# Pooled attention and a top-1 mixture of experts: the routing scratch in another PSUM bank, wider row spacing in the routing table, four buffers of x and two of the exponentials

## The chip, the core and the metric

The kernel runs on one core of a Trainium2 chip. The metric is device time in microseconds (us) of a whole execution.

## What is computed

The reference, cut to what matters:

```
# attention: 8 batches, 8 heads, 576 tokens, 64 per head
k_p = k.reshape(B, H, 72, 8, D).mean(axis=3)      # keys and values are
v_p = v.reshape(B, H, 72, 8, D).mean(axis=3)      # averaged by eights
attn = softmax(q @ k_p.T / 8);  o = attn @ v_p
x = o, as 4608 tokens of 512 numbers
# mixture of experts
out = x.copy()
xc = x[x @ w_skip > 0]                            # about half of the tokens
e_idx, gate_w = top 1 of softmax(xc @ w_gate)     # one of 8 experts
h = relu(xc @ w1[e]);  y = gate_w * (h @ w2[e])   # 512 -> 1024 -> 512
out[computed tokens] = xc + y
```

## The kernel before

**Two stages.** `attention` works through 36 tiles of 128 tokens (the loop at L633), writes each tile's x to `out` in DRAM (L367), and routes the tokens meanwhile. `experts` then takes, for each expert, its tokens out of `out` again, runs the two layers in products of a high and a low half of each number (L1075 to L1093), and scatters the sums back. Between the two, `slots` (L791) works out which tokens each expert gets, in units of 128 slots.

**A tile's way.** The attention is pipelined over the tiles: in the turn of tile t, TensorE does the scores of t (L299), the transposes of the exponentials of t-2 (L324 into the PSUM tile `pt`, L328 into `pr`), and the value products of t-4 (L342, L344) into `o`. VectorE takes the minimum of t's negated scores (L306); ScalarE does eight exponentials of t-1, one for each head (L313), and copies `pt` and `pr` to SBUF (L325, L329); VectorE normalises tile t-5 out of `o` (`rs` L359, `rc` L361, the routing logits L365, x L366), and SyncE issues the transfer of that x to `out` (L367). `x` has three buffers, so the write of a tile's x needs the transfer of the x three tiles before to have landed; `e` (the exponentials) has three as well. `o` is one buffer of two PSUM banks, so the value products of the next tile (L342) wait for L366.

**PSUM.** Eight banks: three for scores, one for `pr`, one (`mps`) that the small jobs share, one for `pt`, two for `o`. The bank of `pr` is cut in two: columns 0 to 255 hold the transposes of L328, columns 256 to 511 are the scratch of the routing. The scheduler orders accesses bank by bank: who writes into `pr` waits for a VectorE access to the scratch, though the columns differ.

**Routing.** `route` (L373) works in six groups of 9, 9, 7, 6, 3 and 2 tiles. VectorE sums the logits of the heads and finds each token's expert, in some ten small operations on the scratch, up to the one-hot `r_oh` (L401). In the next turn ScalarE takes the exponentials of the logits (`r_ex`, L403) and TensorE counts, by products with a triangle and with ones (L407, L409) into an `mps` tile, each token's rank among those of its expert. VectorE adds the running counts (L410, L411) and, one turn on, forms the token's row of the table (`r_di`, L421): expert x 4608 + rank. GpSimd then writes for each tile of the group the pair of token number and gate to these rows, by an indirect DMA of 128 times 8 bytes (L426). Tokens that skip have a row out of bounds and are not written. The table lies in DRAM. After the last group, L842 gathers 128 rows each of it, transposes turn them into the slot numbers (L873, L874), and the first tokens are gathered by these (L876).

**Values of a batch.** `pool_v` (L226) sums values by eights on GpSimd (L234 to L236), transposes the sums (L259, L260) and multiplies them by the gate's weights (L268, L269), both into `mps` tiles, and spreads them into `vbd` and `vl` (L276, L279), which the value products read.

**Order.** On TensorE, ScalarE and VectorE the instructions run in the order in which the program writes them; on GpSimd and on SyncE's queue the scheduler sets the order. `weights` loads expert 0's weights between the tiles and splits them into halves (L550 on ScalarE, the rest L552 on VectorE or L554 on GpSimd). In the last two turns (t = 34 and 35) `tx` (L482) transposes two early tiles of tokens for expert 0, so that its work can begin while the tail of the attention and the routing run out.

The lines in question:

```
side_ps = ps_p.tile([128, 4, 128], F32, name="pr")                      # L186
pr, scratch = side_ps[:, 0:2], flat(side_ps)[:, 256:512]                # L187
rk = flat(ps_m.tile([128, 4, 128], F32, name="mps"))[:, 0:(n + 1) * NE] # L405
m = nc.gpsimd.indirect_dma_start(table, bass.IndirectOffsetOnAxis(ap=di[:, j:j + 1], axis=0),
                                 pay[:, t0 + j, :], None, ...)          # L425
```

Of the kernel before, what the change touches and what calls it, by code (L numbers as in the profile page):

```python
# [26 lines left out]
F32 = mybir.dt.float32  # L27
F32R = mybir.dt.float32r
BF16 = mybir.dt.bfloat16
I32 = mybir.dt.int32  # L30
AF = mybir.ActivationFunctionType
ALU = mybir.AluOpType
# [4 lines left out]
B, H, S, HD, POOL = 8, 8, 576, 64, 8  # L37
SP = S // POOL
D = H * HD
NTOK = B * S  # L40
NT = NTOK // 128
NE, F = 8, 1024
JT = NTOK // 128
MAXU = NT // 2 + NE - 1
UNITS = MAXU + 2
# [57 lines left out]
def flat(ap):  # L103
    return ap.rearrange("p k n -> p (k n)")
# [56 lines left out]
def attention(tc, nc, q, k, vm, vr, cf, w1, w2, whi, wlo, out, c, pay, offs, table, load_constants, near, bufs, late, early, fin):  # L161
    with ExitStack() as ctx:
# [20 lines left out]
        nc.gpsimd.memset(init[:, 512:], 0.0)  # L183
        l8s = {}

        side_ps = ps_p.tile([128, 4, 128], F32, name="pr")  # L186
        pr, scratch = side_ps[:, 0:2], flat(side_ps)[:, 256:512]  # L187

# [37 lines left out]
        def pool_v(b, vt, vl):  # L226
# [28 lines left out]
            for _ in range(SUMS[min(b, 2)]):  # L255
                yield
            tp = ps_m.tile([128, 4, 128], F32, name="mps")
            for j in range(2):
# [5 lines left out]
            if b:  # L264
                yield
            gp = ps_m.tile([128, 512], F32, name="mps")
            for j in range(2):
# [42 lines left out]
        def exped(sc, nm):  # L310
            e = ap.tile([128, H, SP], F32, name="e", bufs=3)
            for h in range(H):
                nc.scalar.activation(e[:, h, :], sc[h // 4][:, h % 4 * SP:(h % 4 + 1) * SP], AF.Exp,  # L313
                                     bias=nm[:, h:h + 1], scale=-1.0)
            return e
# [31 lines left out]
        def normalised(t, os):  # L347
            x = ap.tile([128, H, HD], F32, name="x", bufs=3)
            t0 = max(a for a in starts if a <= t)
# [23 lines left out]
        def route(t0, n):  # L373
# [11 lines left out]
            mx = new("r_mx"); no = new("r_no"); cn = new("r_cn"); oh = new("r_oh", NE, dt=BF16)  # L385
            ex = new("r_ex", NE); sn = new("r_sn"); di = new("r_di", dt=I32)
            nc.vector.tensor_reduce(lp, l8s.pop(t0)[:, :n].rearrange("p j h c -> p j c h"), axis=AX.X, op=ALU.add)
# [16 lines left out]

            rk = flat(ps_m.tile([128, 4, 128], F32, name="mps"))[:, 0:(n + 1) * NE].rearrange("p (j e) -> p j e", e=NE)  # L405
            for j in range(n):
# [13 lines left out]
            yield  # L420
            nc.vector.tensor_tensor(di, ds, no, ALU.add)  # L421
            yield
            nc.vector.reciprocal(pay[:, t0:t0 + n, 1], sn)
# [43 lines left out]
        def tile_steps():  # L467
# [13 lines left out]

            def tx(land, i):  # L482
                ps = flat(ps_t.tile([128, 4, 128], F32, name="pt") if i % 2 else ps_m.tile([128, 4, 128], F32, name="mps"))
                sl = slice(i * 128, i * 128 + 128)
                for k in range(4):
                    nc.tensor.transpose(ps[:, k * 128:k * 128 + 128], land[:, k * 128:k * 128 + 128], ident)
                pv = ps.rearrange("p (k n) -> p k n", k=4)
                nc.scalar.activation(xhi[:, :, sl], pv, AF.Copy)
                return lambda: nc.vector.tensor_tensor(xlo[:, :, sl], pv, xhi[:, :, sl].bitcast(F32), ALU.subtract)
# [143 lines left out]
        for t in range(NT):  # L633
# [35 lines left out]
            if t >= NT - 2:  # L669
                assert not later  # L670
                if t == NT - 2:
                    tx, steps = tile_steps()
                low = tx(bufs["ring"][:, t - NT + 5], t - NT + 2)
            nm = ap.tile([128, H], F32, name="nm")
# [116 lines left out]
def slots(tc, nc, c, offs, table, near, bufs, out, fin, p, psum):  # L791
# [6 lines left out]
    none = new("none"); kind = new("kind"); slim = new("slim")  # L798
    ends = p.tile([128, H, SP], F32, name="e", bufs=3).rearrange("p h k -> p (h k)")[:, 0:UNITS * NE].rearrange("p (u e) -> p u e", e=NE)
    row = p.tile([128, UNITS], F32, name="s_row", bufs=1)  # L800
# [477 lines left out]
```

## Time and profile before

| what | us |
|---|---|
| three runs | 553.86, 556.23, 557.14 |
| median | 556.23 |
| profiled execution | 556.37 |
| its span, first to last instruction | 554.6 |

A profile is of one execution. Its span is 1.8 us shorter than that execution's own time; the rest is start and end around the instructions. PE is TensorE, DVE VectorE, ACT ScalarE, POOL GpSimd, and SP SyncE. A name with a q (SPq, POOLq) is the same engine where it issues transfers. The windows view gives for a stretch of the span its length, the busy time of PE, PE's weight loads, DVE, ACT and POOL with the count of instructions, then the clock that the throttle granted TensorE (1.00 is full speed), the mean busy share of the sixteen DMA engines, and GB/s. A row of the timeline gives start, duration, engine, line, operation, output and inputs; in brackets stands how long the engine had sat idle and who ended that. A row of the waits view says who waited for whose result, and in how many us in all, how many times, and the longest. The view of DMA issues gives count, size and the median time from issue to landing.

### The profile page before, as it was taken

Reading aid. Unit: us, or ns where it says so; the run is one execution under the profiler, and the core shown is the slowest. Engines: PE = TensorE matmul, PEld = TensorE weight load, DVE = VectorE, ACT = ScalarE, POOL = GpSimd, SP = SyncE. Lnnn points to the kernel's source line nnn. Section 1 sums busy time; section 2 is a strip of 40 time slices with the busy share of each in tenths; the row PEclk is TensorE's granted clock in tenths of the full one; section 3 lists DMA queues with packets and bytes.
Section 4 is the critical chain, followed back from the end, with each engine's and each line's share of the span. In section 5 each row is a group of like instructions: output and inputs, shape, how many; then the busy total and the mean of one; then the engine's idle time right before and its main releaser. Section 6 shows DMA issues by size and latency. Waiting matters only on the chain. (4 is left out here: it accounts for less than half of the span.)

```text
span 554.6 us, 11051 instructions
## 1 busy us (share of the span) xinstructions
PE 513.1 (93%) x3346; PEld 460.4 (83%) x3347; DVE 298.7 (54%) x696; ACT 244.7 (44%) x671; POOL 215.7 (39%) x293
## 2 busy tenths in 40 slices
PE   6799997898899969999999999999999999999994
PEld 3699796797788758798989898998989898989893
DVE  4577776876777622235632653233254657565563
ACT  5588796799661112123412341122244445443441
POOL 5764547669836423121422132323232043314042
PEclk8799999999899978999999999999999999999997
DMA  8989899788952011015421442102144637462200
GB/s 292 389 293 338 278 289 262 275 304 167 306 121 76 12 33 48 23 58 173 146 95 57 170 155 78 57 38 68 61 170 144 223 125 272 153 226 100 97 27 7
DMA packets 33591, 86.03 MB, mean 155 GB/s; under 512 B 7501, under 2 KB 7762, under 8 KB 31760
## 3 DMA queue, kind: packets, MB, share of 16 engines
q1 hardware_dynamic: 25456, 71.62, 39.3%
q0 software_dynamic: 8096, 13.95, 7.8%
q8 instruction: 18, 0.29, 0.2%
q14 instruction: 21, 0.17, 0.1%
HBM read 73.79 MB, written 20.52 MB: 170 GB/s over the span
## 5 line engine op out<-in xcount | busy, mean ns | idle before, releaser
L1075 PE MATMUL psl<-xhi,w1hi 128*128 128x256 f32 (+3 forms) x416 | 123.4, 297 | 5.1 <-PEq L905 3.8
L1076 PE MATMUL psl<-xlo,w1hi 128*128 128x256 f32 (+3 forms) x416 | 122.6, 295 | 0.0
L1077 PE MATMUL psl<-xhi,w1lo 128*128 128x256 f32 (+3 forms) x416 | 122.5, 294 | 0.0
L1131 ACT ACTIVATE hhi<-psl 128x256 fp32r<-128x256 f32 (+4 forms) x104 | 42.0, 404 | 159.6 <-ACTq L905 158.5
L994 POOL DMA_INDIRECT out<-ring,slot x39 | 39.7, 1019 | 184.5 <-POOLq L905 173.8
L1090 PE MATMUL psf<-w2hi,hhi 128*128 128x512 f32 x240 | 96.1, 400 | 2.5 <-issue 1.3
L1091 PE MATMUL psf<-w2lo,hhi 128*128 128x512 f32 x240 | 94.9, 395 | 0.0
L1188 DVE SCALAR_TENSOR_TENSOR hlo<-psl,hhi 128x256 fp32r<-128x256 f32 (+2 forms) x104 | 43.8, 423 | 82.0 <-DVEq L905 81.5
L1075 PEld LDWEIGHTS psl<-xhi,w1hi 128*128 128x128 f32 x416 | 79.5, 191 | 7.1 <-issue 6.5
L1076 PEld LDWEIGHTS psl<-xlo,w1hi 128*128 128x128 f32 x416 | 79.6, 191 | 0.5
L1077 PEld LDWEIGHTS psl<-xhi,w1lo 128*128 128x128 f32 x416 | 79.4, 191 | 0.0
L1093 PE MATMUL psf<-w2hi,hlo 128*128 128x512 f32 x200 | 79.1, 395 | 0.0
L313 ACT ACTIVATE e<-sc,nm 128x72 f32<-128x72 f32 x288 | 65.3, 353 | 1.0 <-DVE nm L306 0.8
L1177 DVE SCALAR_TENSOR_TENSOR ring<-psf,ring 128x512 f32 x25 | 18.7, 749 | 78.7 <-DVEq L905 78.7
L342 PE MATMUL o<-vbd,pT 128*128 128x148 f32 (+1 forms) x304 | 49.6, 300 | 6.8 <-DVE x L366 4.2
L1090 PEld LDWEIGHTS psf<-w2hi,hhi 128*128 128x128 f32 x240 | 45.1, 188 | 12.7 <-issue 2.9
L1091 PEld LDWEIGHTS psf<-w2lo,hhi 128*128 128x128 f32 x240 | 45.1, 188 | 9.7
L989 POOL DMA_INDIRECT ring<-out,slot x39 | 45.0, 1154 | 15.6 <-issue 13.4
L1140 ACT ACTIVATE xhi<-psd 128x512 fp32r<-128x512 f32 x36 | 18.9, 598 | 70.5 <-ACTq L905 70.5
L342 PEld LDWEIGHTS o<-vbd,pT 128*128 128x128 f32 (+1 forms) x304 | 41.3, 184 | 8.4 <-issue 4.5
L1093 PEld LDWEIGHTS psf<-w2hi,hlo 128*128 128x128 f32 x200 | 37.6, 188 | 9.1
L426 POOL DMA_INDIRECT table<-pay,r_di x36 | 35.7, 990 | 22.3 <-DVE rc L361 9.9
(218 smaller groups left out, 863.6 us busy)
## 6 DMA issues: line engine op xcount, KB each, us to landing
stage<-in_w SPq DMA_DIRECT2D x64, 512.0 KB, 4.3
out<-x SPq DMA_DIRECT2D x36, 256.0 KB, 5.9
stage<-in_k SPq DMA_DIRECT2D x6, 1152.0 KB, 10.3
hlo<-in_vm SPq DMA_DIRECT2D x4, 1024.0 KB, 7.9
hhi<-in_vm SPq DMA_DIRECT2D x4, 1024.0 KB, 8.4
xlo<-in_q SPq DMA_DIRECT2D x6, 512.0 KB, 8.1
qt<-in_q SPq DMA_DIRECT2D x6, 512.0 KB, 8.1
xhi<-in_q SPq DMA_DIRECT2D x5, 512.0 KB, 12.0
```

What stands on the lines that cost most here:

```text
L313: nc.scalar.activation(e[:, h, :], sc[h // 4][:, h % 4 * SP:(h % 4 + 1) * SP], AF.Exp, bias=nm[:, h:h + 1], scale=-1.0)
L342: nc.tensor.matmul(o_[sl, g * 2 * VA:(g + 1) * 2 * VA], pT[:, 2 * a + g, sl], vbd[b % 3][:, 2 * a + g, :], start=(g == 0), stop=False)
L989: g.indirect_dma_start(ring[:, s % 6, 0:D], None, out, bass.IndirectOffsetOnAxis(ap=slot[:, s:s + 1], axis=0), bounds_check=NTOK - 1, oob_ ...
L994: g.indirect_dma_start(out, bass.IndirectOffsetOnAxis(ap=offsets, axis=0), ring[:, s % 6, 0:D], None, bounds_check=NTOK - 1, oob_is_err=Fa ...
L1075: t.matmul(ps, whi[0][:, k, w], xhi[:, k, xs], start=(k == 0), stop=False)
L1076: t.matmul(ps, whi[0][:, k, w], xlo[:, k, xs], start=False, stop=False)
L1077: last = t.matmul(ps, wlo[0][:, k, w], xhi[:, k, xs], start=False, stop=(k == 3))
L1090: t.matmul(ps, hhi[:, k, sl], whi[1][:, k, :], start=(k == 0), stop=False)
L1091: last = t.matmul(ps, hhi[:, k, sl], wlo[1][:, k, :], start=False, stop=(short and k == 7))
L1093: last = t.matmul(ps, hlo[:, k, sl], whi[1][:, k, :], start=False, stop=(k == 7))
L1131: a.activation(hhi[:, f, xs], psL[f % 3][:, xs], AF.Relu).then_inc(sem["act"], 1)
L1188: m = v.scalar_tensor_tensor(to[:, f], psL[f % 3][:, cs], 0.0, hhi[:, f, cs].bitcast(F32), ALU.max, ALU.subtract)
```

## The change

Four edits:

1. **Banks.** The bank of `pr` now holds the transposes of L328 alone. The routing scratch moves to the bank of `mps`, which becomes one tile, `side_ps`, that lives through the attention: the value batches' transposes lie in its columns 0 to 383, their gate products and the rank products at its start, the routing scratch in the last 180 columns. The early `tx` of the last two turns takes the `pt` bank both times.
2. **Rows of the table.** Each row number is changed by two more VectorE operations for each group: row r becomes r xor ((r mod 4) x 8). A row of 8 bytes moves by 0, 8, 16 or 24 rows, that is by multiples of 64 bytes, so rows that follow each other in rank no longer share 64 bytes; every aligned stretch of 32 rows stays a stretch of the same 32.
3. **Buffers of x:** four instead of three.
4. **Buffers of the exponentials `e`:** two instead of three.

```
-        side_ps = ps_p.tile([128, 4, 128], F32, name="pr")
-        pr, scratch = side_ps[:, 0:2], flat(side_ps)[:, 256:512]
+        pr = ps_p.tile([128, 4, 128], F32, name="pr")[:, 0:2]
+        side_ps = ps_m.tile([128, 512], F32, name="mps")
+        scratch = side_ps[:, 512 - GMAX * 20:]
...
-            tp = ps_m.tile([128, 4, 128], F32, name="mps")
+            tp = side_ps[:, 0:384].rearrange("p (j n) -> p j n", j=3)
...
-            gp = ps_m.tile([128, 512], F32, name="mps")
+            gp = side_ps
...
-            e = ap.tile([128, H, SP], F32, name="e", bufs=3)
+            e = ap.tile([128, H, SP], F32, name="e")
...
-            x = ap.tile([128, H, HD], F32, name="x", bufs=3)
+            x = ap.tile([128, H, HD], F32, name="x", bufs=4)
...
-            rk = flat(ps_m.tile([128, 4, 128], F32, name="mps"))[:, 0:(n + 1) * NE].rearrange(...)
+            rk = side_ps[:, 0:(n + 1) * NE].rearrange(...)
...
             nc.vector.tensor_tensor(di, ds, no, ALU.add)
+            nc.vector.tensor_scalar(dx, di, 3, 3, ALU.bitwise_and, ALU.logical_shift_left)
+            nc.vector.tensor_tensor(di, di, dx, ALU.bitwise_xor)
...
-            def tx(land, i):
-                ps = flat(ps_t.tile(..., name="pt") if i % 2 else ps_m.tile(..., name="mps"))
+            def tx(land, i, early=False):
+                ps = flat(ps_t.tile(..., name="pt") if early or i % 2 else ps_m.tile(..., name="mps"))
```

The order on TensorE, ScalarE and VectorE stays, apart from the new operations on VectorE; the semaphores that instructions wait on change with the banks, and GpSimd's order moves in places. TensorE in the turn in which the first routing group does its first steps on VectorE, before (names: `pt` and `pr` take the transposes of the exponentials, `cfs` holds the identity, `kbd` the keys, `vbd` and `vl` the values):

```order
L324 MATMUL pt<-cfs,e 128x128 [waits Activation_49]
L324 MATMUL pt<-cfs,e 128x128 x3
L328 MATMUL pr<-cfs,e 128x128 [waits DVE_49,Activation_49]
L328 MATMUL pr<-cfs,e 128x128
L299 MATMUL sc<-kbd_115,xlo 128x144 [waits Activation_49]
L299 MATMUL sc<-kbd_115,xlo 128x144
L342 MATMUL o<-vbd_123,pT 128x148 [waits DVE_49,PE_49]
```

The same place with the change, where every line number from here on is one higher or more:

```order
L325 MATMUL pt<-cfs,e 128x128 [waits Activation_49]
L325 MATMUL pt<-cfs,e 128x128 x3
L329 MATMUL pr<-cfs,e 128x128 [waits Activation_49]
L329 MATMUL pr<-cfs,e 128x128
L300 MATMUL sc<-kbd_115,xlo 128x144 [waits DVE_49,Activation_49]
L300 MATMUL sc<-kbd_115,xlo 128x144
L343 MATMUL o<-vbd_123,pT 128x148 [waits DVE_49,PE_49]
```

The transposes into `pr` have lost their wait on VectorE; the second half of the scores, which follows them, now names VectorE itself. Later in the same turn and into the next come the rank products on TensorE, before:

```order
L344 MATMUL o<-vl_126,p_791 128x148
L299 MATMUL sc<-kbd_115,xlo 128x144 [waits Activation_49]
L299 MATMUL sc<-kbd_115,xlo 128x144
L407 LDWEIGHTS ones
L407 MATMUL mps<-r_oh,ones 128x80 [waits DVE_49]
```

And with the change:

```order
L345 MATMUL o<-vl_126,p_787 128x148
L300 MATMUL sc<-kbd_115,xlo 128x144 [waits Activation_49]
L300 MATMUL sc<-kbd_115,xlo 128x144
L408 LDWEIGHTS ones
L408 MATMUL mps<-r_oh,ones 128x80 [waits Activation_49]
```

The first rank product waited on VectorE, which writes the one-hot `r_oh`; it now waits on ScalarE, whose `r_ex` (L403) reads the scratch in the bank into which the product writes. The third place is GpSimd at the sums of value batch 6 (`hlo` and `vl` hold the loaded values, `w1lo` the low half of a weight chunk), before:

```order
L279 TENSOR_TENSOR vl_125<-gs,cfs 64x4x9 [waits Activation_49]
L234 TENSOR_TENSOR hlo<-hlo 128x256 [waits DMAHW4_49]
L234 TENSOR_TENSOR hlo<-hlo 128x256 x3
L234 TENSOR_TENSOR vl<-vl 64x256 [waits DMAHW5_49]
L235 TENSOR_TENSOR hlo<-hlo 128x512 [waits Pool_49]
L235 TENSOR_TENSOR vl<-vl 64x128 [waits Pool_49]
L554 TENSOR_TENSOR w1lo<-stage,w1hi 128x512 [waits DMAHW1_49,Activation_49]
L236 TENSOR_TENSOR vs<-hlo 128x256 [waits PE_49,Pool_49]
```

And with the change:

```order
L280 TENSOR_TENSOR vl_125<-gs,cfs 64x4x9 [waits Activation_49]
L558 TENSOR_TENSOR w1lo<-stage,w1hi 128x512 [waits DMAHW1_49,Activation_49]
L235 TENSOR_TENSOR hlo<-hlo 128x256 [waits DMAHW4_49]
L235 TENSOR_TENSOR hlo<-hlo 128x256 x3
L235 TENSOR_TENSOR vl<-vl 64x256 [waits DMAHW5_49]
L236 TENSOR_TENSOR hlo<-hlo 128x512 [waits Pool_49]
L236 TENSOR_TENSOR vl<-vl 64x128 [waits Pool_49]
L237 TENSOR_TENSOR vs<-hlo 128x256 [waits PE_49,Pool_49]
```

The split of a weight chunk into halves (L554, L558 with the change) now stands ahead of the batch's sums instead of among them. The other moves are of the same kind: a low half of w2 between the sums of batch 7, one scatter of the first group ahead of a low half of w2.

More of the change, by code (lines that the diff above doesn't have):

```diff
@@ L385, in route @@
             mx = new("r_mx"); no = new("r_no"); cn = new("r_cn"); oh = new("r_oh", NE, dt=BF16)
-            ex = new("r_ex", NE); sn = new("r_sn"); di = new("r_di", dt=I32)
+            ex = new("r_ex", NE); sn = new("r_sn"); di = new("r_di", dt=I32); dx = new("r_dx", dt=I32)
             nc.vector.tensor_reduce(lp, l8s.pop(t0)[:, :n].rearrange("p j h c -> p j c h"), axis=AX.X, op=ALU.add)
@@ L403, in route @@
             nc.scalar.activation(ex, l, AF.Exp)
-            rk = flat(ps_m.tile([128, 4, 128], F32, name="mps"))[:, 0:(n + 1) * NE].rearrange("p (j e) -> p j e", e=NE)
+            rk = side_ps[:, 0:(n + 1) * NE].rearrange("p (j e) -> p j e", e=NE)
             for j in range(n):
@@ L480, in bank @@
                 return hold["ps"]
-            def tx(land, i):
-                ps = flat(ps_t.tile([128, 4, 128], F32, name="pt") if i % 2 else ps_m.tile([128, 4, 128], F32, name="mps"))
+            def tx(land, i, early=False):
+                ps = flat(ps_t.tile([128, 4, 128], F32, name="pt") if early or i % 2 else ps_m.tile([128, 4, 128], F32, name="mps"))
                 sl = slice(i * 128, i * 128 + 128)
@@ L672, in attention @@
                     tx, steps = tile_steps()
-                low = tx(bufs["ring"][:, t - NT + 5], t - NT + 2)
+                low = tx(bufs["ring"][:, t - NT + 5], t - NT + 2, True)
             nm = ap.tile([128, H], F32, name="nm")
@@ L798, in slots @@
     none = new("none"); kind = new("kind"); slim = new("slim")
-    ends = p.tile([128, H, SP], F32, name="e", bufs=3).rearrange("p h k -> p (h k)")[:, 0:UNITS * NE].rearrange("p (u e) -> p u e", e=NE)
+    ends = p.tile([128, H, SP], F32, name="e").rearrange("p h k -> p (h k)")[:, 0:UNITS * NE].rearrange("p (u e) -> p u e", e=NE)
     row = p.tile([128, UNITS], F32, name="s_row", bufs=1)
```

## Prediction

> **What bounds the kernel now.** I read the page first, for the shares of the engines.
>
> ```profile
> span 554.6 us, 11051 instructions
> PE 513.1 (93%) x3346; PEld 460.4 (83%) x3347; DVE 298.7 (54%) x696; ACT 244.7 (44%) x671; POOL 215.7 (39%) x293
> ```
>
> TensorE is the engine that sets the time: busy for 513.1 of 554.6 us, the next one for 298.7. So an edit is worth what it takes from TensorE's idle time or slow time. The windows tell the two stages apart.
>
> ```profile
> 0.00:204.70 204.70, 175.61 (x1302) 155.99 (x1303) 138.51 (x425) 130.06 (x475) 121.04 (x175) 0.95 0.73 233
> 204.70:554.60 349.90, 337.49 (x2044) 304.38 (x2044) 160.20 (x271) 114.68 (x196) 94.66 (x118) 0.98 0.32 110
> ```
>
> The change touches the first stage alone. There TensorE is idle for 204.7 - 175.6 = 29.1 us, and its clock is 0.95 instead of the 0.98 of the second stage. Next, the waits, of which these are TensorE's in the middle of the stage.
>
> ```profile
> PE o L342 <- DVE x L366: 4.2, 1, 4.2
> ...
> PE pr L328 <- DVE l L365: 2.7, 3, 1.0
> PE pr L328 <- DVE rs L359: 2.7, 2, 1.4
> PE o L342 <- POOL vbd L276: 2.6, 1, 2.6
> PE pr L328 <- DVE pr L410: 2.3, 2, 1.6
> ```
>
> One wait of 4.2 us on the normalised x, one of 2.6 us on GpSimd's values, and seven waits of the transposes into `pr` on VectorE, 2.7 + 2.7 + 2.3 = 7.7 us in all. The change is aimed at the first and the third.
>
> **Four buffers of x.** The timeline shows what stood behind the 4.2 us, and the line of the transfers says how old it was.
>
> ```profile
> 94.36 0.69 DVE L366 TENSOR_TENSOR x<-o,rc 128x512 f32<-128x512 f32 x1 [4.57 <-DMA out<-x]
> ...
> 95.20 0.83 PE L342 MATMUL o<-vbd,pT 128*128 128x148 f32 x2 [4.16 <-DVE x L366]
> ```
>
> ```profile
> L367 SPq DMA_DIRECT2D out<-x x1: 344/344/344, 79.5 to 79.5; - x1
> ...
> DMA to landing us min/median/max: 14.8/14.8/14.8
> ```
>
> VectorE wanted to write x at 94.36 - 4.57 = 89.8 and had to wait for the transfer issued at 79.5, which landed at 79.5 + 14.8 = 94.3. With four buffers this write needs an older transfer, and the wait is gone. Late next is the write one tile on, which now needs the transfer that lands at 94.3. How long a tile takes is in the row of all x writes of this stretch.
>
> ```profile
> L366 DVE TENSOR_TENSOR x<-o,rc x16: 680/681/692, 63.8 to 127.3; 128x512 f32<-128x512 f32 x16
> ```
>
> Fifteen turns in 63.5 us, less the stall of 4.2 and some 1.5 of slow clock (below), are 3.85 us each. The next write comes at 89.8 + 3.85 = 93.65 and waits 0.65. VectorE had 0.4 us to spare ahead of TensorE (4.57 against 4.16), so 0.25 of that reaches TensorE. The stall gives 4.16 - 0.25 = 3.9 us. It also drags the clock:
>
> ```profile
> 91.40:94.80 3.40, 0.00 (x0) 0.00 (x0) 0.44 (x1) 1.04 (x3) 2.76 (x7) 1.00 0.93 217
> 94.80:98.20 3.40, 3.00 (x12) 2.97 (x12) 2.24 (x5) 1.69 (x6) 0.00 (x0) 0.50 1.01 400
> 139.20:142.60 3.40, 0.80 (x7) 0.68 (x6) 3.15 (x4) 2.23 (x9) 3.40 (x6) 1.00 0.77 220
> 142.60:146.00 3.40, 3.40 (x16) 3.39 (x15) 3.30 (x8) 0.00 (x0) 3.02 (x3) 0.50 0.99 337
> ```
>
> After 3.4 us without a matmul the clock is 0.50 for the next 3.4 us, in which 3.00 us of busy time are worth 1.5. With the stall gone that is 1.5 us more: the edit gives 5.4. Its bounds: 2.5, if another transfer is late by 2 us or more in place of this one and the slow clock stays, and 5.7, if nothing waits.
>
> The last two rows show the same after the stall on `vbd`, with 0.80 us of work in the window before. The Trainium skill (TensorE: Matmul & The Clock Gate, Part 1, What's actually happening) says that the slow clock follows on one whole idle window of about 3.4 us, of a grid that runs free. By that rule the rows at 139.2 would have brought no slow clock; the trace shows 0.50 after 2.6 idle us, so the measurement decides.
>
> For the sum it matters that such windows start every 3.4 us while everything after 95 us now comes some 5 us earlier. The stall on `vbd` can fall otherwise into them, and its slow clock (1.7) go; or another pause can catch one. I take no change, and 1.7 either way as a bound.
>
> **The bank of `pr` alone.** It removes VectorE's waits ahead of L328, 7.7 us. But see what TensorE does after such a wait.
>
> ```profile
> 104.02 0.68 DVE L366 TENSOR_TENSOR x<-o,rc 128x512 f32<-128x512 f32 x1
> 104.11 0.41 PE L328 MATMUL pr<-cfs,e 128*128 128x128 f32 x2 [0.96 <-DVE l L365]
> ...
> 104.85 0.35 PE L342 MATMUL o<-vbd,pT 128*128 128x148 f32 x1
> ```
>
> The transposes had waited 0.96. Then follow the scores, and L342 at 104.85, which cannot start before L366 has ended, at 104.02 + 0.68 = 104.70. Had L328 started 0.96 earlier, L342 would still have waited for 104.70: gain 0.15. The longest wait, 1.62, ends so:
>
> ```profile
> 109.43 0.16 DVE L411 TENSOR_TENSOR offs<-offs,mps 128x8 f32<-128x8 f32 x1
> 109.45 0.44 PE L328 MATMUL pr<-cfs,e 128*128 128x128 f32 x2 [1.62 <-DVE pr L410]
> 109.74 0.41 PE L259 MATMUL mps<-cfs,vs 128*128 128x128 f32 x2
> ```
>
> L259, right behind, writes `mps`, which L411 reads until 109.59: it would stop there, 0.15 earlier than now. The other five are of the same kind: they stand in turns in which VectorE is late with its routing steps, and the next value products wait for VectorE's x in any case. I count 0.3 for all seven; the bounds are 0 and 7.7, and the two that can be followed, with 0.3 of 2.58, are near the lower.
>
> **The new wait.** The rank products write into the bank that ScalarE reads for `r_ex`, so they now come behind it, as the order shows. Before, of the first three groups:
>
> ```profile
> 66.56 0.28 ACT L403 ACTIVATE r_ex<-pr 128x72 f32<-128x72 f32 x1
> 66.68 0.37 PE L407 MATMUL mps<-r_oh,ones 128*128 128x80 bf16 x8
> ```
>
> ```profile
> 106.92 0.40 PE L407 MATMUL mps<-r_oh,ones 128*128 128x80 bf16 x9
> 107.04 0.29 ACT L403 ACTIVATE r_ex<-pr 128x72 f32<-128x72 f32 x1
> ```
>
> ```profile
> 136.68 0.34 PE L407 MATMUL mps<-r_oh,ones 128*128 128x64 bf16 x7
> 137.66 0.27 ACT L403 ACTIVATE r_ex<-pr 128x56 f32<-128x56 f32 x1
> ...
> 141.92 0.64 PE L342 MATMUL o<-vbd,pT 128*128 128x148 f32 x3 [2.60 <-POOL vbd L276]
> ```
>
> `r_ex` ended 0.16 after the start of the products in the first group (66.84 against 66.68), 0.41 in the second and 1.25 in the third. TensorE's queue stands behind the rank products: the transposes of the exponentials first. The first two cost 0.16 + 0.41 plus some 0.1 each for the hand-over, 0.8; the third is swallowed by the 2.60 that TensorE waits for `vbd` five us later. The last three groups, at the end of the stage, are led by VectorE, which both sides wait for. So 0.8 lost; the bounds are 0 and, with all three and the last groups as bad as the third, 6 x 1.25 = 7.5.
>
> **The two operations on the rows.** The nearest row is the step that they follow, of the last group:
>
> ```profile
> 180.34 0.16 DVE L421 TENSOR_TENSOR r_di<-r_room,r_no 128x2 int32<-128x2 f32 x1 [0.54 <-DMA table<-pay,r_di]
> ```
>
> They work on as few numbers, so two times 0.16 for each group. In five of them VectorE has time to spare by the end of the turn; in the last, the scatters and the gather of the slots wait for it: 0.3 lost.
>
> **What the row spacing does to the transfers.** This the trace of before can only bound. The median landing times of the first two groups' nine scatters and of those at the end, by the DMA issues in three stretches, and two windows while scatters are under way:
>
> ```profile
> table<-pay,r_di POOLq DMA_INDIRECT x9, 10.4
> ```
>
> ```profile
> table<-pay,r_di POOLq DMA_INDIRECT x9, 8.0
> ```
>
> ```profile
> table<-pay,r_di POOLq DMA_INDIRECT x9, 5.0
> ```
>
> ```profile
> 88.00:94.00 6.00, 3.04 (x25) 2.73 (x24) 1.72 (x5) 4.12 (x16) 5.92 (x10) 1.00 1.07 147
> 124.00:130.00 6.00, 6.00 (x50) 5.76 (x49) 4.89 (x12) 6.00 (x25) 4.90 (x6) 1.00 0.58 18
> ```
>
> Between 124 and 130 us the DMA engines are busy for 0.58 of the time to move 18 GB/s; from 94.8 to 98.2, above, they moved 400 GB/s at 1.01. So these small writes hold the engines for long, and it is such a stretch (88 to 94: full, at 147 GB/s) in which the transfer of 79.5 is late. If writes into the same 64 bytes get in each other's way, the spacing lets them land sooner. With four buffers only 0.25 us of x's wait is left to gain, and the 0.54 for which L421 waits at 180.34: 0.8 at most on this path. I take 0, since no row shows two spacings. The Trainium skill (DMA: Bandwidth & Descriptors, Specifications) speaks against this edit: below 512 bytes every write is a read, a change and a write. By that rule each row stays one such write wherever it lies, the spacing gives nothing, and the two operations are a pure loss; the sum below is by 0 as well.
>
> **Edits at nothing.** With two buffers of `e`, the exponentials of a tile wait for the transposes two tiles back, which stand ahead of them in TensorE's order by a whole turn. The early `tx` in `pt` takes a bank that ScalarE has emptied by then. GpSimd's `w1lo`, now ahead of batch 6's sums, takes this long:
>
> ```profile
> 105.95 1.26 POOL L554 TENSOR_TENSOR w1lo<-stage,w1hi 128x512 fp32r<-128x512 f32 x1
> ```
>
> It was among the sums before, so what comes behind them comes no later, as long as ScalarE's `w1hi` is there when GpSimd arrives; if not, the sums wait, and a `vbd` behind them can come late to L342. The cover is the slack of that `vbd`, whose wait shows once (2.6) in this half of the stage; without it the edit costs up to 1.3.
>
> **The sum.** 3.9 + 1.5 + 0.3 - 0.8 - 0.3 = 4.6 us less. The profiled execution took 556.37 us, 554.6 of span and 1.8 around it; its like becomes 551.8. The median of 556.2 lies 0.1 below it, so 551.8 is the forecast for the median too, 0.8% faster.
>
> **Rivals.** What a measurement of this kernel can tell from no change is about 0.5%, 2.8 us.
>
> *The transfers come free, and the clock with them.* The scatters land sooner, x and L421 never wait (0.8), and the stall on `vbd` no longer takes a window of the clock (1.7): 551.8 - 2.5 = 549.3. For it speaks the window of 18 GB/s at 0.58; against it, that GpSimd is busy for all of the window from 139.2 to 142.6, and so the stall on `vbd` is its own.
>
> *GpSimd keeps what x gives.* A run of scatters, halves of weights and sums on GpSimd leads up to the `vbd` that ends the wait at 141.92. It starts here:
>
> ```profile
> 117.90 1.02 POOL L426 DMA_INDIRECT table<-pay,r_di  x1 [0.15 <-DVE x L366]
> ```
>
> If its start is held by a weight chunk or a landing that doesn't come earlier, TensorE arrives at L342 sooner and waits for the same 141.9: the 3.9 are lost there again, only the 1.5 of clock and some tenths stay, 556.4 - 1.5 = 554.9. For it: 2.60 us of wait stand there now. Against: what GpSimd waited for at its start is VectorE's, which moves with TensorE.
>
> *Slower: the rank products behind the exponentials.* `r_ex` stands in ScalarE's queue behind the exponentials of a tile, eight of them:
>
> ```profile
> 139.82 1.80 ACT L313 ACTIVATE e<-sc,nm 128x72 f32<-128x72 f32 x8 [0.20 <-DVE nm L306]
> ```
>
> If TensorE waits for all of them in each of the six groups, that is 6 x 1.8 = 10.8 instead of 0.8: 551.8 + 10.0 = 561.8. It decides from 0.9 us for each group on, where the gain of 5.4 is used up. The third group's 1.25 is above this, the first two's 0.16 and 0.41 are far below.
>
> **How the numbers follow.** The forecast has 0.45, the freed transfers 0.25, GpSimd 0.22, the rank products 0.08. Below, the range takes in 549.3 and 1.8 more for the pr waits being worth more than 0.3: 547.5. Above, it takes in GpSimd's 554.9 and 0.6 for `vbd`'s cover: 555.5. Left out are most of the slower case and the far ends, under 0.2. Faster by over 0.5% (under 553.4) are the first two and a little of the third, 0.72; within it the rest of the third and some of the last, 0.20; slower 0.08.
>
> **What would show it.** Right: no wait of L342 on L366 above 0.5 us, no clock of 0.50 near 95 us, the waits of L328 on VectorE gone while as much stands ahead of L342 or L259, rank products that wait under 0.5 us for ScalarE. The spacing: landing of the scatters near 5 us or still 8 to 10. Wrong: a wait on `vbd` of 6 us, rank products that wait over 0.9 each, or a first stage that ends 8 us or more earlier, for then the waits of L328 were not covered.

## The result, and the profile after

The changed kernel takes 547.73 us (median of 10 runs, 545.65 to 552.93), the kernel before 556.68 beside it (10 runs, 553.46 to 562.13). The ratio is 0.9862, with a 95% interval of 0.9828 to 0.9896: 7.7 us less, between 5.8 and 9.6. (It is not the quotient of the two medians, which lie 8.95 apart; the differences below go by the ratio.) The forecast was 4.6 less, which has the sign and the order, and lies below the interval. The median lies 0.2 above the lower end of the range, 547.5.

The profiled execution of the changed kernel took 550.47 us, 2.7 above the median of its kind. Its page:

```profile
span 548.7 us, 10999 instructions
PE 511.0 (93%) x3346; PEld 459.1 (84%) x3347; DVE 298.4 (54%) x708; ACT 244.3 (45%) x671; POOL 215.6 (39%) x293
```

The same two stages, cut where the first product of the second begins, at 201.05 us instead of 204.73:

```profile
0.00:201.05 201.05, 174.72 (x1303) 155.89 (x1304) 138.28 (x437) 129.71 (x475) 121.15 (x175) 0.96 0.74 237
201.05:548.70 347.65, 336.32 (x2044) 303.25 (x2044) 160.08 (x271) 114.59 (x196) 94.41 (x118) 0.99 0.33 111
```

The first stage is 3.7 us shorter. The second, in which nothing was changed, is 2.2 shorter as well, at a clock of 0.99 instead of 0.98; more of that below. The write of x that had waited 4.57 us, and the one after it:

```profile
89.77 0.68 DVE L367 TENSOR_TENSOR x<-o,rc 128x512 f32<-128x512 f32 x1
...
94.36 0.69 DVE L367 TENSOR_TENSOR x<-o,rc 128x512 f32<-128x512 f32 x1 [0.77 <-DMA out<-x]
```

```profile
91.40:94.80 3.40, 3.06 (x25) 2.34 (x23) 2.56 (x7) 3.36 (x13) 3.32 (x5) 1.00 0.84 198
94.80:98.20 3.40, 3.40 (x32) 3.13 (x31) 3.17 (x7) 3.39 (x13) 0.64 (x3) 1.00 1.11 312
```

The first waits no more, the next waits 0.77 where 0.65 was worked out, and the clock stays at 1.00 through the time in which it had been 0.50. The x after these windows comes at 99.07 instead of 104.02: 4.95 us earlier, where 5.4 were forecast for this edit. But TensorE has new waits:

```profile
PE o L343 <- DVE x L367: 4.9, 3, 3.0
...
PE mps L408 <- ACT r_ex L404: 3.2, 2, 2.0
```

The 3.2 are the rank products behind `r_ex`, 1.23 in the third group and 1.98 in the fifth; for the first two groups, in which the prediction counted the loss, the profile lists none. The longest of the others, 3.0, is new too, and it starts at one of the two small operations that were counted at 0.16 us each. The timeline of VectorE, GpSimd and TensorE there:

```profile
109.89 3.01 DVE L424 TENSOR_SCALAR r_dx<-r_di 128x9 int32<-128x9 int32 x1
...
109.92 1.26 POOL L558 TENSOR_TENSOR w1lo<-stage,w1hi 128x512 fp32r<-128x512 f32 x1
111.14 0.30 POOL L277 TENSOR_TENSOR vbd<-gs,cfs 128x72 f32<-128x72 f32 x1
111.41 0.24 POOL L280 TENSOR_TENSOR vl<-gs,cfs 64x36 f32<-64x36 f32 x1
111.62 1.26 POOL L558 TENSOR_TENSOR w2lo<-stage,w2hi 128x512 fp32r<-128x512 f32 x1
...
114.57 1.28 PE L343 MATMUL o<-vbd,pT 128*64 128x148 f32 x6 [3.00 <-DVE x L367]
```

`r_dx` on 9 numbers a partition lasts 3.01 us, and ends as GpSimd's run does, at 112.88; the four operations shown are the end of a run without a pause since 102.34. In the third group `r_dx` takes 0.86, in the other four 0.17. Here it makes x late, and x the value products, and the clock follows:

```profile
114.50:117.90 3.40, 3.33 (x24) 3.22 (x24) 0.78 (x4) 1.80 (x8) 2.49 (x4) 0.50 1.01 298
```

The median landing times of the scatters, in the same three stretches of the kernel (10.4, 8.0 and 5.0 before):

```profile
table<-pay,r_di POOLq DMA_INDIRECT x9, 9.0
```

```profile
table<-pay,r_di POOLq DMA_INDIRECT x9, 6.3
```

```profile
table<-pay,r_di POOLq DMA_INDIRECT x9, 3.4
```

They are shorter in this profile. That the spacing does it is not shown. A second profile of the changed kernel has 10.6, 5.9 and 3.6, and the changed kernel without the row spacing, below, 10.9, 6.1 and 4.3: the second stretch fell as much without it.

### The profile page after: what moved, and what is told of

Same layout as the page of the kernel before. It is cut to its first block, busy times and chain, and to the rows that moved or that the text cites. A ratio compares the mean times of both kernels' runs of the same rounds, so it can differ in the third digit from the quotient of the medians.

```text
span 548.7 us, 10999 instructions
## 1 busy us (share of the span) xinstructions
PE 511.0 (93%) x3346; PEld 459.1 (84%) x3347; DVE 298.4 (54%) x708; ACT 244.3 (45%) x671; POOL 215.6 (39%) x293
## 6 DMA issues: line engine op xcount, KB each, us to landing
stage<-in_k SPq DMA_DIRECT2D x6, 1152.0 KB, 11.7
xhi<-in_q SPq DMA_DIRECT2D x5, 512.0 KB, 10.9
```

## The experiments

Ratios are to the kernel before on the same chip, with their 95% intervals; the us are the ratio's distance from 1 times that median (555.9 for the first four, 557.5 for the next four).

### Buffers alone

```
 kernel before
-            x = ap.tile([128, H, HD], F32, name="x", bufs=3)
+            x = ap.tile([128, H, HD], F32, name="x", bufs=4)
-            e = ap.tile([128, H, SP], F32, name="e", bufs=3)
+            e = ap.tile([128, H, SP], F32, name="e")
```

> The kernel before with four buffers of x and two of the exponentials, nothing else. Theory A (the prediction): this edit alone gives 5.4 us, about 551 against 556.5, ratio 0.990; VectorE's wait on the transfer of x near 90 us falls from 4.6 to under 0.8, and no clock of 0.50 follows near 95 us. Rival C (the spacing is needed, since the transfer after the late one is late as well): 2 us or less, about 554.5, with a wait on a transfer of x of 2 us or more left in place of the one removed. Where the gain is above 7 us, the buffers are the whole of the change and both are wrong.

Measured: 550.46 us, 0.9900 (0.9864 to 0.9935), 5.6 us less. The two writes of x, and then TensorE at the `vbd` of batch 6:

```profile
89.77 0.68 DVE L366 TENSOR_TENSOR x<-o,rc 128x512 f32<-128x512 f32 x1
...
95.39 0.69 DVE L366 TENSOR_TENSOR x<-o,rc 128x512 f32<-128x512 f32 x1 [1.39 <-DMA out<-x]
```

```profile
138.05 1.35 PE L342 MATMUL o<-vbd,pT 128*128 128x148 f32 x4 [3.65 <-POOL vbd L276]
```

Theory A's size, without help from the row spacing; C's remaining wait of 2 us isn't there, only 1.39, somewhat more than the 0.8 that A allowed. The wait on `vbd`, 2.60 before, is now 3.65: GpSimd has taken back 1.05 of what x gave. Its run up to that `vbd` begins with this scatter, which started at 117.90 before:

```profile
114.07 1.02 POOL L426 DMA_INDIRECT table<-pay,r_di  x1 [0.17 <-DVE nplace L449]
```

This is 3.83 us earlier, while x of that turn is 4.92 earlier (112.21 against 117.13). The difference of 1.09 is about the 1.05.

### Row spacing alone

```
 kernel before
             nc.vector.tensor_tensor(di, ds, no, ALU.add)
+            nc.vector.tensor_scalar(dx, di, 3, 3, ALU.bitwise_and, ALU.logical_shift_left)
+            nc.vector.tensor_tensor(di, di, dx, ALU.bitwise_xor)
```

> The kernel before with the two operations that move the table's rows, nothing else. Theory A: the spacing gives nothing that the path feels; the operations cost 0.3 us, and up to 3 more where the first of them is held up by GpSimd, as it is for 3.01 us in the profile of the changed kernel: 556.5 to 559, ratio 1.000 to 1.005. The scatters land 1.5 us sooner in the median. Rival C (the spacing frees the transfers): the late transfer of x is late no more, the wait of 4.6 us is gone or under 1, about 552, ratio 0.992.

Measured: 558.21 us, 1.0042 (1.0013 to 1.0071), 2.3 us more. The late x:

```profile
92.73 0.69 DVE L366 TENSOR_TENSOR x<-o,rc 128x512 f32<-128x512 f32 x1 [3.13 <-DMA out<-x]
```

The wait on the transfer of x is 1.4 us shorter than before and remains, so C falls. That the spacing made it shorter is not shown: with the banks alone, below, and rows as before, the same wait is 5.22. Nor does the profile show where the 2.3 us come from. Its execution is the fastest of twelve, 5.1 below their median; its first stage is only 0.16 longer than before (204.89 against 204.73), and no `r_dx` in it lasts over 0.73.

### Banks alone

```
 changed kernel
-            x = ap.tile([128, H, HD], F32, name="x", bufs=4)
+            x = ap.tile([128, H, HD], F32, name="x", bufs=3)
-            e = ap.tile([128, H, SP], F32, name="e")
+            e = ap.tile([128, H, SP], F32, name="e", bufs=3)
-            nc.vector.tensor_scalar(dx, di, 3, 3, ...)
-            nc.vector.tensor_tensor(di, di, dx, ALU.bitwise_xor)
```

> The kernel before with the routing scratch in the bank of the small jobs, the transposes of the exponentials alone in theirs, and the early transposes of tokens in the bank of the exponentials' transposes; three buffers of x and three of the exponentials, rows as before. Theory A (the prediction): 0.3 us won by the waits of the transposes, 0.8 lost by the rank products: 556.5 to 557.5, ratio 1.000 to 1.002. Rival B (the waits of the transposes, 7.7 us in all, are not covered): 3 us or more won, 553.5 or less, ratio 0.994 or less, and the turns of the routing groups are shorter by more than a tenth of a us.

Measured: 553.69 us, 0.9953 (0.9925 to 0.9980), 2.6 us less, between 1.1 and 4.2. Theory A falls in its sign; B's 3 us are inside the interval. The profile of this execution can't show where they come from. Its first stage ends at 205.39, 0.66 later than before, and it is shorter in the second alone. B's other sign, shorter turns of the routing groups, isn't there: the turn in which the second group adds its counts takes 6.00 us from x to x, 5.87 before. Two transfers of x were late in it, one of them more than before:

```profile
95.20 0.69 DVE L367 TENSOR_TENSOR x<-o,rc 128x512 f32<-128x512 f32 x1 [5.22 <-DMA out<-x]
```

```profile
132.09 0.69 DVE L367 TENSOR_TENSOR x<-o,rc 128x512 f32<-128x512 f32 x1 [2.84 <-DMA out<-x]
```

### The change without the row spacing

The changed kernel without the same two operations, four buffers of x and two of the exponentials kept.

> The changed kernel without the two operations that move the table's rows, so that the rows lie 8 bytes apart as before. Theory A: the spacing gives nothing, and without its operations the kernel is faster by 0.3 us in any case and by up to 4 where the 3.01 us and the slow clock behind them are spared: 544 to 547.5 against 547.7, ratio to the kernel before 0.978 to 0.985. Rival C (the spacing gives the 3 us by which the prediction was short): 550 to 551.5, ratio 0.989 to 0.991.

Measured: 548.41 us, 0.9867 (0.9823 to 0.9910), 7.4 us less; the whole change has 0.9862. C falls once more. A's range is missed too, by a little: the 3.01 us of `r_dx`, gone here, don't show in the time. Beside the buffers alone (0.9900), this run has only the banks in addition. TensorE in the turn of the second routing group shows whether the transposes' waits were covered. Buffers alone, VectorE's x and then TensorE:

```profile
99.78 0.68 DVE L366 TENSOR_TENSOR x<-o,rc 128x512 f32<-128x512 f32 x1
```

```profile
99.88 0.41 PE L328 MATMUL pr<-cfs,e 128*128 128x128 f32 x2 [0.98 <-DVE l L365]
...
100.62 0.73 PE L342 MATMUL o<-vbd,pT 128*128 128x148 f32 x4
```

Buffers and banks:

```profile
99.61 0.68 DVE L367 TENSOR_TENSOR x<-o,rc 128x512 f32<-128x512 f32 x1
```

```profile
100.44 0.74 PE L343 MATMUL o<-vbd,pT 128*128 128x148 f32 x4 [0.99 <-DVE x L367]
```

The 0.98 at the transposes became 0.99 at the value products, which start 0.83 us after x in both kernels. Here the wait was covered, as the prediction had it. One turn later VectorE adds the counts. Buffers alone, then buffers and banks (`w1lo` is the low half of a weight chunk on VectorE, two operations):

```profile
102.07 2.19 DVE L552 TENSOR_TENSOR w1lo<-stage,w1hi 128x512 fp32r<-128x512 f32 x2
...
104.54 0.44 PE L328 MATMUL pr<-cfs,e 128*128 128x128 f32 x2 [0.94 <-DVE pr L410]
```

```profile
101.81 1.82 DVE L553 TENSOR_TENSOR w1lo<-stage,w1hi 128x512 fp32r<-128x512 f32 x2
...
104.10 0.44 PE L260 MATMUL mps<-cfs,vs 128*128 128x128 f32 x2 [0.32 <-DVE offs L412]
```

The 0.94 became 0.32, and the turn, from x to x, 4.74 us instead of 5.19. But both products wait for VectorE's counts, and of the 0.45 by which they come sooner 0.37 are `w1lo`, which took less. The other place where this kernel gains on the buffers alone is the write of x near 95 us, which waits 0.62 for a transfer instead of 1.39. Neither gain is a wait on the bank of `pr` that went. The first stage ends at 199.80 here and at 200.76 with the buffers alone.

### The changed kernel again

No edit.

> The changed kernel once more, beside the three that follow, for a second profile and a ratio from the same chip as theirs. Theory D (the operation r_dx, a VectorE operation on SBUF alone, is held while GpSimd works, and whether it meets GpSimd there differs between executions): r_dx of the second group takes 0.17 us or anything up to 4; ratio to the kernel before 0.983 to 0.990.

Measured: 549.42 us, 0.9850 (0.9813 to 0.9888). `r_dx` of the second group is held for 3.01 us in this profile as well, and the others again take 0.86 once and 0.17. That it differs between executions, which D allowed, is seen in neither; two executions can't exclude it.

### r_dx in PSUM

`cm` is a part of the routing scratch that is free by then.

```
 changed kernel
+            dx = cm.bitcast(I32)
             nc.vector.tensor_scalar(dx, di, 3, 3, ALU.bitwise_and, ALU.logical_shift_left)
```

> The changed kernel with r_dx in the routing scratch in PSUM instead of SBUF, the same two operations. Theory D: no r_dx above 0.4 us in any group, the wait of the value products on x behind it (3.0 us in the changed kernel's profile) is gone, with the slow clock behind it: 1 to 4 us less than the changed kernel, 544 to 547. Rival E (r_dx is held by something else, a wait on a transfer or on the queue before it): it takes 3 us here too, and the time is the changed kernel's within 1 us.

Measured: 549.20 us, 0.9870 (0.9831 to 0.9909). The operation, and then TensorE at `vbd` and the x behind it:

```profile
109.53 0.17 DVE L425 TENSOR_SCALAR mps<-r_di 128x9 int32<-128x9 int32 x1
```

```profile
136.66 1.35 PE L343 MATMUL o<-vbd,pT 128*128 128x148 f32 x4 [3.91 <-POOL vbd L277]
```

```profile
135.20 4.09 DVE L461 TENSOR_SCALAR nslot<-nids,less 128x2 int32<-128x2 f32 x1 [1.54 <-DMA nids<-table]
140.03 0.17 DVE L360 TENSOR_SCALAR rs<-o 128x8 f32<-128x8 f32 x1 [0.74 <-PE o L345]
...
140.63 0.68 DVE L367 TENSOR_TENSOR x<-o,rc 128x512 f32<-128x512 f32 x1
```

D is right about the operation, 0.17 instead of 3.01, and E falls. But D was wrong about the time. What is spared at 110 us is lost at 137: TensorE, further ahead, waits 3.91 for GpSimd's `vbd`, which the changed kernel's profile doesn't have among TensorE's waits. At 132 us x is 6.0 ahead of the changed kernel's (132.25 against 138.26), at the next x 2.1 (140.63 against 142.70), and at the end of the stage 0.4 (200.67 against 201.05). Another VectorE operation, `nslot`, is held for 4.09 in the same turn, as it was for 4.21 in the kernel before; but VectorE then still idles 0.74 for TensorE, so it isn't `nslot` that sets this x.

### r_ex behind the rank products, alone and with r_dx in PSUM

```
 changed kernel
-            nc.scalar.activation(ex, l, AF.Exp)
...
+            nc.scalar.activation(ex, l, AF.Exp)
```

> The changed kernel with the exponentials of the logits (r_ex) written behind the rank products instead of ahead of them, so that ScalarE waits for TensorE and not TensorE for ScalarE. Theory A: the rank products' wait on r_ex, 3.2 us in the changed kernel's profile, is gone; what TensorE did not wait for anyway comes back, 0.8 to 1.5 us, and less where VectorE's x is late in the same turn: 546 to 547.5. Rival F (ScalarE's wait puts the exponentials of the tile late and TensorE waits for them instead): no gain or up to 1 us more, 547.5 to 549, with the transposes into pt waiting for e.

Measured: 550.98 us, 0.9871 (0.9833 to 0.9910). With both edits:

> The changed kernel with both of these edits: r_dx in PSUM, r_ex behind the rank products. Theories A and D: the gains add, 543.5 to 546, ratio to the kernel before 0.977 to 0.981. If E and F hold, 547.5 to 549.

Measured: 550.04 us, 0.9870 (0.9839 to 0.9902). Neither median shows A's 0.8 to 1.5 us, but intervals of about 2 us to either side can't exclude them. In the profile of the first edit alone they are there: from the x at 77.34 to the one at 142.90, behind the third group's rank products, it takes 65.56 us, and the changed kernel 67.17 for the same tiles (75.53 to 142.70). In place of the wait on `r_ex`, with the first edit alone:

```profile
PE mps L406 <- DVE r_oh L402: 1.9, 1, 1.9
```

And with both:

```profile
PE o L343 <- POOL vbd L277: 5.4, 1, 5.4
```

The longer of the two waits on `r_ex` stood over a wait on VectorE's `r_oh` of almost the same size, in a late group where VectorE leads. With both edits, what was won at the other adds to the wait on `vbd`.

### Work taken off GpSimd

Theory G comes from these: between about 101 and 137 us GpSimd works almost without a pause, and what is won before is lost at its `vbd`. The kernel with r_dx in PSUM, and the low half of w1's last chunk on VectorE:

```
-WPOOL = 3
+WPOOL = 4
```

> The kernel with r_dx in PSUM, and the low half of w1's last chunk (two operations of 1.27 us) on VectorE instead of GpSimd. Theory G (from 101 us on GpSimd works without a pause up to the vbd that ends the wait near 137 us, so what is won before it is lost there): vbd comes some 2.5 us sooner, the wait of the value products on it falls from 3.9 to 1.5 or less, 546 to 547.5 against some 549 for r_dx in PSUM alone. Rival H (VectorE is as late, its nslot held by GpSimd, and x then takes the place of vbd): the wait on vbd falls, a wait on x of the same size stands there, no gain beyond 0.5 us.

The kernel with r_dx in PSUM, and instead of the edit on w1:

```
-                less = ap.tile([128, 1], F32, name="less")
+                less = side_ps[:, 320:321]
-                nc.vector.tensor_scalar(near["slot"], near["ids"][:, :, 0], less, None, ALU.add)
+                nc.vector.tensor_tensor(near["slot"], near["ids"][:, :, 0], less.broadcast_to([128, 2]), ALU.add)
```

> The kernel with r_dx in PSUM, and nslot (VectorE, 128x2, held for 3 to 4 us by GpSimd near 137 us) with its second input in PSUM and as an operation of two tensors. Theory D (one input and the output in SBUF, no second: not held): nslot takes 0.2 us. Theory G: TensorE still waits 3.9 us for vbd in that turn, so the time is that of r_dx in PSUM alone within 0.7 us, 548.5 to 549.5. Rival H (VectorE's held nslot is what delays the turn): 2 to 4 us less, 545 to 547.

All four edits together:

> The four edits together: r_dx in PSUM, r_ex behind the rank products, the low half of w1's last chunk on VectorE, nslot with one input in PSUM. Theories D and G: no operation of VectorE held for 2 us or more, the wait on vbd 2.5 us shorter than the 5.4 it was with the first two edits, 544.5 to 547, ratio to the kernel before 0.977 to 0.983. If G does not hold, 548.5 to 550, as with the first two.

Measured: 567.55 us, 0.9920 (0.9887 to 0.9953); 571.14, 0.9987 (0.9964 to 1.0010); 568.07, 0.9915 (0.9885 to 0.9945). On this chip the kernel before took 571.84 (29 runs), 15 us more than on the others, and the profiles have stops of TensorE, VectorE and ScalarE together that no other has, as here with the first of the three:

```profile
80.00:84.00 4.00, 0.29 (x3) 0.10 (x2) 1.20 (x4) 0.00 (x0) 3.09 (x4) 0.98 0.91 315
```

What stops them the profile doesn't name. The three kernels can be compared with one another: taking the two operations off GpSimd is worth 3.8 us against the edit of `nslot`, clear of both intervals. But with TensorE late by the stops, the wait on `vbd` is in none of the three profiles, so this says nothing on G. With the edit of `nslot`, this operation was not held there, though GpSimd's `w2lo` ran from 152.12 to 153.39 beside it:

```profile
L461 DVE TENSOR_TENSOR nslot<-nids,mps x1: 144/144/144, 152.3 to 152.3; 128x2 int32<-128x2 f32 x1
```

The first of the three again, on another chip:

> The kernel with r_dx in PSUM and the low half of w1's last chunk on VectorE once more, since the kernel before took 572 us on the chip of the last three runs and 556 to 558 on the others, with stops of all engines near 80 us that the other profiles do not have. Where the kernel before takes 554 to 559: theory G, ratio to it 0.979 to 0.984 (545 to 548), and no wait on vbd above 1.5 us near 137 us; rival H, 0.986 to 0.988 as with r_dx in PSUM alone, with a wait on x of 2 to 4 us in the place of vbd's.

Measured: 548.43 us against 558.09, 0.9843 (0.9794 to 0.9891). TensorE's longest waits on VectorE, and VectorE where the moved operations run and where x ended up:

```profile
PE o L343 <- DVE x L367: 3.6, 4, 1.5
```

```profile
106.43 1.57 DVE L557 TENSOR_TENSOR w1lo<-stage,w1hi 128x512 fp32r<-128x512 f32 x1
...
112.06 1.40 DVE L557 TENSOR_TENSOR w1lo<-stage,w1hi 128x512 fp32r<-128x512 f32 x1
...
140.60 0.68 DVE L367 TENSOR_TENSOR x<-o,rc 128x512 f32<-128x512 f32 x1
```

The wait on `vbd` is down to 0.2, which is G's. But x of that turn is at 140.60, where it was at 140.63 with r_dx in PSUM alone: VectorE now carries the two operations and is late by as much, which is H's. The next x is 1.1 earlier than with r_dx in PSUM alone (143.81 against 144.88) and the first stage ends at 198.01 instead of 200.67, so in this one profile H holds for that turn and not for the stage. The ratio lies between the two expectations, and its interval holds both, and the changed kernel's. No version that is clearly faster than the changed kernel was found.

## Why the prediction was right and where it was wrong

**Four buffers of x: right in place, and in size within the interval.** 5.4 forecast, 5.6 (3.6 to 7.6) measured with this edit alone. The wait that goes, what is late next and the slow clock that goes are in the profile as worked out; the sizes are less close. The next write waits 1.39 instead of 0.65, of which 0.71 instead of 0.25 reach TensorE, and the first stage ends 3.97 earlier (200.76 against 204.73), not 5.4. The other 2.8 us between the two profiles lie in the second stage, where nothing was changed. That 5.6 agrees so closely with 5.4 is in part luck.

**The bank of `pr` and the new wait: wrong in sign.** The step that failed is "I count 0.3 for all seven" against "So 0.8 lost": a net loss of 0.5 was forecast, a gain of 2.6 (1.1 to 4.2) was measured with this edit alone, and 1.8 in the difference between 0.9867 and 0.9900, whose intervals overlap. This is about the 3 us by which the forecast was short: -5.6 and -2.6 add up to -8.2, and 7.4 to 7.7 were measured together. Of the loss, the two groups that made it up show no wait in the changed kernel's profile. The third waits 1.23, as was read, and there its cover, the wait on `vbd`, is gone; the fifth waits 1.98, over a wait on VectorE's `r_oh` of 1.9, as was said of the last groups. Of the gain, neither of the two turns that can be compared shows a wait on `pr` that was worth more than forecast. A part of the 2.6 may be clock: its mean is 0.976 over the twelve runs with the banks alone and 0.973 over the 25 before, and these 25 differ by 2.8 us for 0.01 of clock, which gives an estimate of 0.8 us. The early `tx` is an unlikely cause, since its waits are the same (2.4 us in all before and in the changed kernel). GpSimd's order, which this edit also moves, was not tried apart. The cause of this gain stays open.

**A term at nothing: how long VectorE's `w1lo` takes.** The turn in which the second group adds its counts was counted at a gain of 0.15. From x to x it takes 5.87 us before (104.02 to 109.89) and 4.34 with the change (99.07 to 103.41). VectorE has no pause in it, and one item differs by more than 0.1:

```profile
106.30 2.87 DVE L552 TENSOR_TENSOR w1lo<-stage,w1hi 128x512 fp32r<-128x512 f32 x2
```

```profile
101.27 1.28 DVE L556 TENSOR_TENSOR w1lo<-stage,w1hi 128x512 fp32r<-128x512 f32 x2
...
102.34 2.85 POOL L235 TENSOR_TENSOR hlo<-hlo 128x256 f32<-128x256 f32 x4 [1.35 <-DMA hlo<-in_vm]
```

The same two operations take 1.28 where GpSimd waits for a transfer most of that time, and 2.87 where it works throughout. The turn follows them in each kernel: 4.74 us with 1.82 (buffers and banks), 5.19 with 2.19 (buffers alone), 6.00 with 3.08 (banks alone), 6.76 with 3.76 (spacing alone). So 1.5 us of the lead in the changed kernel's profile come from this, which no term of the sum had. What sets GpSimd's work beside it was not tried.

**The row spacing: right that the path feels nothing, wrong in its price.** The operations were counted at 0.3. Alone, the edit costs 2.3 (0.7 to 3.9); in its profile the turn above is 0.9 longer than before. In the changed kernel the first of them is held for 3.01 us, and still the ratio with and without them is the same within the intervals, 0.9862 and 0.9867, for the reason that follows. Whether the scatters land sooner is not settled: the median of the first nine is 9.0 to 10.7 us in the profiles with spaced rows and 10.4 to 11.7 in those without, the three kernels with the stops left out. The rule that below 512 bytes each write is a read, a change and a write (the Trainium skill, DMA: Bandwidth & Descriptors, Specifications), by which the spacing gives nothing, is not contradicted by these runs.

**GpSimd keeps what x gives: a rival at 0.22, and partly so.** It was held against it that what GpSimd waits for moves with TensorE. It does for the most part (3.83 of 4.92 us with the buffers alone), yet between there and `vbd` GpSimd has its own work and no pause, and TensorE's wait on `vbd` grew from 2.60 to 3.65 with the buffers alone, and to 3.91 and 5.4 with r_dx in PSUM and with both edits. So it kept 1 us of the buffers' gain, and most of what r_dx in PSUM won before it (6.0 us became 2.1). In the profiles this is why the repair of `r_dx`, right about its operation, shows no gain; for `r_ex` alone no wait on `vbd` stands there, and its gain is only too small for these intervals.

**The rank products behind the exponentials:** 1.23 and 1.98 us in two of six groups, 3.2 in all. This rival was to decide from 0.9 in each of the six, 5.4 in all; it didn't come.

**The signs that were named.** Two of the signs of being right did not come: the value products waited 3.0 on x behind `r_dx`, where no wait above 0.5 was expected, and two groups of rank products waited over 0.9, which was named as a sign of being wrong. Two others came: no slow clock near 95 us, and no wait of the transposes into `pr` on VectorE. That the time still lies in the range, by 0.2 us, is less than the spread of the runs, and the range reached that far down for transfers that come free and for waits on `pr` worth more, neither of which the runs show as a cause. This is luck.

## What to carry to other kernels

A wait that goes is worth what is not late next, and this has to be followed over the next engine's whole run, not for one turn: here GpSimd's unbroken work up to one tile took back most of what was won 30 us earlier. A VectorE operation that reads and writes SBUF is costed with what GpSimd does at that moment (0.17 or 3.01 us, 1.28 or 2.87); with its output in PSUM `r_dx` took its own 0.17. And a saving of a few us is measured in many executions of each kernel, since a profiled one lay 2.7 us above the median here (the changed kernel) and 5.1 below it there (the spacing alone). Even six to twelve leave about 2 us to either side.

## What the runs showed of the hardware

**VectorE held by GpSimd.** `r_dx`, an operation of one tensor from SBUF to SBUF, took 3.01 us beside GpSimd's run and 0.17 with its output in PSUM; `nslot` took 4.09 as such an operation, and 0.144 as one of two tensors with one of them in PSUM. A held operation ends with GpSimd's run of operations, however many are in it: `r_dx` at 112.90 against 112.88, `nslot` at 139.29 against 139.26, and in the kernel before at 144.56 against 144.52. The Trainium skill (SBUF — State Buffer, Who interferes with whom) says that a tensor_scalar between SBUF operands can take the port pair that VectorE shares with GpSimd, and that whoever comes second is fully blocked. The trace agrees for `r_dx` in that it is blocked until GpSimd stops.

**The clock without any change of work.** The second stage is the same code in all kernels, and its profiles differ by 4.4 us: 349.9 in the kernel before and 345.5 with the banks alone. The first windows of that stage, before:

```profile
204.70:208.10 3.40, 3.37 (x16) 3.39 (x17) 0.00 (x0) 0.32 (x1) 2.82 (x5) 0.50 0.05 9
208.10:211.50 3.40, 3.40 (x20) 3.40 (x20) 0.85 (x2) 0.45 (x2) 1.91 (x3) 0.59 0.56 140
```

And with the banks alone:

```profile
205.40:208.80 3.40, 3.40 (x29) 3.40 (x30) 0.42 (x1) 0.62 (x2) 2.90 (x5) 1.00 0.09 16
208.80:212.20 3.40, 3.40 (x31) 3.40 (x31) 1.15 (x3) 0.92 (x3) 1.82 (x3) 1.00 0.49 154
```

TensorE is full in all four from its first product on; in one execution it starts the stage at half clock for almost two windows, in the other not. The pause ahead of the stage is the same:

```profile
204.73 0.56 PE L1075 MATMUL psl<-xhi,w1hi 128*128 128x256 f32 x1 [3.09 <-PEq L905]
```

```profile
205.39 0.37 PE L1076 MATMUL psl<-xhi,w1hi 128*128 128x256 f32 x1 [3.13 <-PEq L906]
```

That what differs is where the pause falls among the clock's windows is argued from this and not shown by a run. Over the ten runs of the changed kernel, times from 545.65 to 552.93 go with mean clocks from 0.991 to 0.971, the shorter times mostly with the higher clocks. The Trainium skill (TensorE: Matmul & The Clock Gate, Part 1, What's actually happening) has these windows run free of the kernel, which fits.
